# Attention steps placed by a list scheduler inside the kernel, with more of the splits on GpSimd

## Chip, core and metric

The kernel runs on one core of a Trainium2 chip. The metric is device time in microseconds (us) of one execution. The engines are TensorE (PE, its weight loads PEld), VectorE (DVE), ScalarE (ACT), GpSimd (POOL) and SyncE (SP, which issues nearly all DMAs here).

## The reference

```python
scores = (q @ k.T) / 8                       # batch 4, 8 heads, 576 x 576, head size 64
scores = where(scores >= max(scores) - tau, scores, -1e9)
attn = exp(scores - max(scores)); attn /= sum(attn) + 1e-9
x = attn @ v                                 # as 2304 tokens x 512
x = (silu(x @ w_gate) * (x @ w_val)) @ w_out        # inner width 1536
out = ((x @ w1) * (x @ w2) @ w3) @ w_out2           # inner width 1024
```

All inputs are float32. Products are made in a rounded format, so each operand is split into a rounded part hi and a remainder lo, and two or three products are added.

## The kernel before

The program has two stretches. The first is attention; the second, the two feed-forward blocks, is not touched.

Attention goes over 16 pairs of heads (p = 0 to 15), and a pair over nine score tiles (i = 0 to 8). For a tile, `mm_scores` multiplies four times (eight for i = 4) into one of two PSUM score banks (`s_bank`). `el_tile` then runs, on DVE, the pass L473, which copies the tile to SBUF as E and accumulates its extreme, the small add L477, which adds tau to that extreme (128x1, both inputs in SBUF), and the pass L481, which masks by the threshold and writes P (E comes from SBUF, the other input from the score bank). The exponential L485 follows on ACT. A score bank is free again after L481.

From P, ten banks of a pair are turned: four by `it_T(p, 0, c)`, one each by `it_lq` and `it_kl`, four by `it_T(p, 1, c)`. A turn is four transposes on PE (L327) into one of four `t_bank`s. `evac_split` takes hi and lo out of the bank by one of three paths: X (ACT copies hi, DVE subtracts, L505 and L507), Z (ACT copies hi L497, PE subtracts hi in the bank L334, ACT copies lo L501), Y (ACT copies the bank to SBUF L518, POOL rounds it L102 and subtracts L105). The paths come in rotation, `PATHS = "XZYXZZYXZ"`. A small corner bank goes by ACT and DVE.

`it_pv` multiplies the values, once for each head and half: eight products with `AT` (L566) and two with `ATL` (L571) into one bank, all ten emitted together; ACT copies the result (L578), and SP stores it (L582). AT and ATL exist once, so a pair's turns into them wait for the value products of the pair before.

For the next pair, `turn` transposes q and k; ACT takes hi (L342), DVE lo (L344), and `stack` (L350, L351) issues 12 DMAs on SP, eight for L (q) and four for R (k), which the next pair's scores read. `it_left` prepares the left-over rows.

The order comes from two queues of closures: before and after each tile, `some(0.5)` takes closures from `main` and `prep` by credits.

```python
def some(frac):
    credit[0] += 19.5 / 9 * frac
    credit[1] += (1.5 if in_tail else 1.0) * frac
    for c, qu in ((1, prep), (0, main)):
        while credit[c] >= 1 and qu:
            credit[c] -= 1
            run_item(qu.popleft())
```

The instructions emitted so are placed on the engines by the framework's own scheduler, which may change their order. Three early weight conversions (pairs 3, 6, 9) also run in this stretch.

Of the kernel before, what the change touches and what calls it, by code (L numbers as in the profile page):

```python
# [30 lines left out]

PATHS, LAST = "XZYXZZYXZ", "XZ"


@with_exitstack
def kernel(
# [62 lines left out]
    def split_pool(hi, lo, src):  # L101
# [2 lines left out]
        )  # L104
        nc.gpsimd.tensor_tensor(out=lo, in0=src, in1=f32(hi), op=ALU.subtract)  # L105

    def split_act_pool(hi, lo, src):
        nc.scalar.copy(out=hi, in_=src)  # L108
        nc.gpsimd.tensor_tensor(out=lo, in0=src, in1=f32(hi), op=ALU.subtract)  # L109
# [20 lines left out]
        nc.sync.dma_start(out=dst, in_=src)  # L130
        return raw

    def conv_bits(raw):
# [16 lines left out]
        nc.scalar.activation(out=a, in_=x, func=ACTF.Relu, scale=8.0, bias=ebias[:, 0:1])  # L150
        nc.scalar.activation(out=x, in_=x, func=ACTF.Relu, scale=-8.0, bias=ebias[:, 1:2])  # L151
        nc.gpsimd.tensor_tensor(out=a, in0=a, in1=x, op=ALU.subtract)  # L152
        return a, m

    def conv_value(bits):
        if wide == 1:
            return bits
        a, m = bits
# [76 lines left out]
    def attention(actx, early, tail):  # L235
# [23 lines left out]
        def load_left(b):  # L259
            qk = ld.tile([P, H, D], F32, tag="qkl", name="qkl", bufs=1)  # L260
            vl = ld.tile([P, HP, D], F32, tag="vl", name="vl", bufs=1)
            nc.sync.dma_start(out=qk[0:64], in_=q[b, :, 512:S, :].rearrange("h p d -> p h d"))
            nc.sync.dma_start(out=qk[64:128], in_=k[b, :, 512:S, :].rearrange("h p d -> p h d"))
            vs = v[b, :, 512:S, :].rearrange("(g e) p d -> e p g d", e=2)
            for e in range(2):
                nc.sync.dma_start(out=vl[64 * e:64 * e + 64], in_=vs[e])
            lraw[b] = (qk, vl)

        def load(p, which):
            b, hp = divmod(p, HP)  # L270
            for i in which if p < NP else ():
                src = (q, k, v)[i][b, 2 * hp:2 * hp + 2, 0:512, :]
                if i == 2:
                    t = wk.tile([P, 2, 4, D], F32, tag="ld2", name="ld2")
                    nc.sync.dma_start(out=t, in_=src.rearrange("h (p t) d -> p h t d", t=4))
                else:
                    t = ld.tile([P, 4, 2, D], F32, tag=f"ld{i}", name=f"ld{i}")
                    if p == 0:
                        t = t.rearrange("p (h a) b d -> p h (a b) d", h=2)
                        nc.sync.dma_start(out=t, in_=src.rearrange("h (p t) d -> p h t d", t=4))  # L280
                    else:
                        nc.sync.dma_start(out=t, in_=src.rearrange("h (p t) d -> p t h d", t=4))
                raws[p, i] = t
# [167 lines left out]
        def p_tile(p, i):  # L451
            if (p, 0) not in pbuf:
                for t in range(4):
                    pbuf[p, t] = pb[p % 2].tile([P, 2 * S], F32, tag=f"P{t}", name=f"P{t}")
                pbuf[p, 4] = pb[p % 2].tile([P, S], F32, tag="P4", name="P4")
            if i == 4:
                return pbuf[p, 4]
            h, t = (0, i) if i < 4 else (1, i - 5)
            return pbuf[p, t][:, h * S:(h + 1) * S]
# [4 lines left out]
                sums[b] = wk.tile([P, NSM], F32, tag="sums", name="sums")  # L464
            return stats[b]

        def el_tile(p, i, sb):
            st = stat(p // HP)
            c = slice(col_of(p, i), col_of(p, i) + 1)
            src = sb[:, :, 0:HALF]  # L470
            halves = lambda t: t.rearrange("p (a c) -> p a c", a=2)
            t = wk.tile([P, S], F32, tag="E", name="E", bufs=N_E)
            nc.vector.tensor_scalar(  # L473
                out=halves(t), in0=src, scalar1=-FAR, scalar2=None,
                op0=ALU.mult, op1=ALU.min, accum_out=st[:, 0, c],
            )
# [4 lines left out]
            nc.vector.scalar_tensor_tensor(  # L481
                out=halves(u), in0=halves(t), scalar=st[:, 1, c], in1=src,
                op0=ALU.is_gt, op1=ALU.subtract,
            )
            nc.scalar.activation(  # L485
                out=u, in_=u, func=ACTF.Exp, scale=-FAR, bias=st[:, 0, c],
                accum_out=sums[p // HP][:, c],
            )


        path_i = [0]

        def evac_split(hi, lo, bank):
            path = LAST[path_i[0] % len(LAST)] if in_tail else PATHS[path_i[0] % len(PATHS)]
            path_i[0] += 1
            if path == "Z":
                nc.scalar.copy(out=hi, in_=bank)  # L497

                def rest():
                    less(bank, hi)  # L500
                    nc.scalar.copy(out=lo, in_=bank)  # L501

                deferred.append(rest)
            elif path == "X":
                nc.scalar.copy(out=hi, in_=bank)  # L505
                deferred.append(
                    lambda: nc.vector.tensor_tensor(  # L507
                        out=lo, in0=bank, in1=f32(hi), op=ALU.subtract
                    )
                )  # L510
            else:
                raw = tmp()
                rv = raw
                if len(bank.shape) == 3:
                    rv = raw.rearrange("p (a c) -> p a c", a=bank.shape[1])
                if len(bank.shape) == 4:
                    rv = raw.rearrange("p (c h q) -> p c h q", c=4, h=2)
                nc.scalar.copy(out=rv, in_=bank)  # L518
                if path == "Y":
                    split_pool(hi, lo, rv)  # L520
                else:
                    nc.scalar.copy(out=hi, in_=bank)
                    nc.gpsimd.tensor_tensor(out=lo, in0=rv, in1=f32(hi), op=ALU.subtract)
# [89 lines left out]
        def split_items(p):  # L613
            return [lambda: split_left(p // HP)] if p % HP == 0 else []
# [46 lines left out]
        def stage_s(n):  # L661
            if n < NS:
                banks[n] = mm_scores(*tiles[n])

        def stage_el(n):
# [4 lines left out]
            if i == 8:  # L670
                main.extend(b_items(p))

        credit = [0.0, 0.0]

        def some(frac):
            credit[0] += 19.5 / 9 * frac
            credit[1] += (1.5 if in_tail else 1.0) * frac
# [3 lines left out]
                    run_item(qu.popleft())  # L681
                credit[c] = min(credit[c], 1.0)

        stage_s(0)
        stage_s(1)
        for n, (p, i) in enumerate(tiles):
            b, hp = divmod(p, HP)
            if i == 0:
                if p + 2 < NP:
                    if (p + 2) % HP == 0:  # L690
                        load_left((p + 2) // HP)
                    load(p + 2, (1, 0))
                while prep:
                    run_item(prep.popleft())
                if p + 1 < NP:
                    prep.extend(prep_items(p + 1))
                    credit[1] = 0.0 if p else -1.5
            if i == NTILE - 2:
                while prep:
                    run_item(prep.popleft())  # L700
                if p + 2 < NP:
                    prep.extend(split_items(p + 2))
            some(0.5)
            stage_el(n)
            stage_s(n + 2)
            some(0.5)
            if i == 4 and p in EARLY:
                prep.extend([conv_step, conv_end])
            if n + NTILE == NS:
                in_tail.append(True)  # L710
                lctx.close()
                prep.extend(early())
            if n + 2 == NS:
                while main:
                    run_item(main.popleft())
                qctx.close()
                prep.extend(tail())
# [382 lines left out]
```

## Time and profile before

| what | value |
|---|---|
| median of three runs | 1192.82 us (1192.11 to 1193.11) |
| profiled execution | 1192.23 us, span 1190.4 us |
| granted TensorE clock, mean | 0.987 |
| busy share of the span: PE, PEld, DVE, ACT, POOL | 94%, 80%, 63%, 50%, 32% |
| first L473 of pair 2, of pair 15 | 56.33 us, 340.51 us |

Busy time is the union of an engine's instructions; "idle before" is the time in which the engine did nothing before an instruction, and the arrow names what ended it. Inside an engine, consecutive instructions overlap a little, so a step from start to start can be shorter than a duration.

### The profile page before, as it was taken

The page shows a single profiled execution, that of the slowest core. Times are in us where ns is not written, and L with a number is a line of the kernel's source. Part 1 is how long each engine was busy: PE and PEld are TensorE (multiplying, and loading weights), DVE is VectorE, ACT ScalarE, POOL GpSimd, SP SyncE. Part 2 cuts the span into 40 slices and gives each one's busy share as a digit, 9 for nine tenths or more (in the row PEclk, how much of TensorE's full clock was granted, in tenths as well). Part 3 has the DMA queues.
Part 4 walks back from the last instruction along what each step waited for, and adds up shares of the span by engine and source line. Part 5 has one row for each costly group of instructions (what it writes and reads, how often), then busy time and mean ns, then how long its engine had stood idle before and what let it go on. Part 6 is the DMA issues. An engine that isn't in the chain of part 4 may idle for free.

```text
span 1190.4 us, 16901 instructions
## 1 busy us (share of the span) xinstructions
PE 1124.1 (94%) x6044; PEld 955.8 (80%) x6044; DVE 753.5 (63%) x1319; ACT 596.5 (50%) x1187; POOL 384.4 (32%) x353
## 2 busy tenths in 40 slices
PE   5998888899889889999999999999899999999998
PEld 4887778787777678888888888888787888888886
DVE  6888898889987797666464564577892022432222
ACT  4888888888876546443242432345563331321111
POOL 3234233233232655444232342234241131321210
PEclk9999999999998999999999999999899999999999
DMA  9675665665545653222021120123330010100014
GB/s 208 153 159 141 145 166 130 155 141 122 123 138 144 198 151 108 88 71 70 20 71 36 36 89 1 53 83 109 120 111 22 1 36 1 36 1 1 1 57 103
DMA packets 105331, 107.09 MB, mean 90 GB/s; under 512 B 48288, under 2 KB 79648, under 8 KB 105248
## 3 DMA queue, kind: packets, MB, share of 16 engines
q1 hardware_dynamic: 105104, 106.01, 33.4%
q8 instruction: 48, 0.79, 0.3%
q14 instruction: 35, 0.29, 0.1%
q10 hardware_dynamic: 144, 0.00, 0.0%
HBM read 68.16 MB, written 14.23 MB: 69 GB/s over the span
## 4 chain that ended last, share of the span: by engine, by line
PE 71%; DVE 15%; ACT 5%; DMA 3%; issue 3%; SPq 1%; POOL 0%; DVEq 0%; ACTq 0%; POOLq 0%
PE t_bank L804 37%; PE s_bank L804 19%; PE t_bank L566 5%; PE s_bank L441 5%; PE t_bank L327 3%; DVE E L473 3%; DVE P L481 2%; DMA raw<-in_moe_w_dram 2%; DVE slot L787 2%; ACT P L485 1%; DVE stat L477 1%; PE t_bank L571 1%; DVE raw L144 1%; DVE tmp L147 1%; DVE tmp L159 1%
## 5 line engine op out<-in xcount | busy, mean ns | idle before, releaser
L804 PE MATMUL t_bank<-slot,slot 128*128 128x512 f32 (+1 forms) x2592 | 561.2, 371 | 5.0 <-DVE slot L787 2.8
L804 PEld LDWEIGHTS t_bank<-slot,slot 128*128 128x128 f32 x2592 | 457.4, 189 | 92.4 <-DVE slot L787 4.0
L804 PE MATMUL s_bank<-h,slot 128*128 128x512 f32 (+1 forms) x720 | 164.1, 376 | 3.6 <-ACT h L108 2.9
L804 PEld LDWEIGHTS s_bank<-h,slot 128*128 128x128 f32 x720 | 128.4, 192 | 28.5 <-ACT h L108 3.4
L152 POOL TENSOR_TENSOR raw<-raw 128x512 int32<-128x512 int32 x76 | 83.3, 1096 | 170.8 <-ACT raw L151 157.8
L1036 DVE TENSOR_TENSOR tmp<-tmp,t_bank 128x512 f32<-128x512 f32 (+1 forms) x40 | 25.3, 633 | 178.2 <-PE t_bank L804 178.2
L473 DVE TENSOR_SCALAR_CACHE_REDUCE E<-s_bank 128x576 f32<-128x576 f32 x144 | 107.0, 752 | 32.9 <-PE s_bank L441 32.2
L485 ACT ACTIVATE P<-P,stat 128x576 f32<-128x576 f32 x144 | 113.5, 789 | 23.9 <-DVE P L481 23.4
L109 POOL TENSOR_TENSOR h<-tmp,h 128x512 fp32r<-128x512 f32 (+1 forms) x60 | 75.6, 1260 | 141.9 <-ACT h L108 137.0
L481 DVE SCALAR_TENSOR_TENSOR P<-E,stat,s_bank 128x576 f32<-128x576 f32 x144 | 114.5, 808 | 1.5
L441 PE MATMUL s_bank<-R,L 128*128 128x288 f32 x512 | 99.0, 317 | 16.0 <-DVE P L481 10.9
L327 PE MATMUL t_bank<-ident,P 128*128 128x128 f32 x640 | 98.4, 282 | 14.6 <-ACT P L485 7.8
L1040 POOL TENSOR_TENSOR h<-tmp,h 128x512 fp32r<-128x512 f32 (+1 forms) x38 | 45.8, 1205 | 200.5 <-ACT h L1038 200.5
L804 PE MATMUL s_bank<-slot,h 128*128 128x512 f32 x432 | 106.6, 391 | 0.9 <-DVE slot L1026 0.8
L889 DVE TENSOR_TENSOR tmp<-tmp,t_bank 128x512 f32<-128x512 f32 (+1 forms) x60 | 37.9, 631 | 108.2 <-PE t_bank L804 101.1
L441 PEld LDWEIGHTS s_bank<-R,L 128*128 128x128 f32 x512 | 76.3, 195 | 27.5 <-issue 9.4
L327 PEld LDWEIGHTS t_bank<-ident,P 128*128 128x128 f32 x640 | 75.8, 143 | 27.0 <-ACT P L485 14.0
L804 PEld LDWEIGHTS s_bank<-slot,h 128*128 128x128 f32 x432 | 80.0, 188 | 18.3 <-DVE slot L1026 2.1
L851 DVE TENSOR_TENSOR slot<-s_bank,slot 128x1024 f32<-128x1024 f32 (+1 forms) x72 | 82.4, 1146 | 18.6 <-PE s_bank L804 16.5
L159 DVE SCALAR_TENSOR_TENSOR tmp<-tmp,raw 128x512 f32<-128x512 f32 x76 | 68.2, 899 | 33.4 <-POOL raw L152 33.3
L888 ACT ACTIVATE tmp<-t_bank 128x512 f32<-128x512 f32 (+1 forms) x60 | 33.3, 555 | 109.7 <-PE t_bank L804 103.3
L150 ACT ACTIVATE raw<-raw,ebias 128x512 int32<-128x512 int32 x76 | 58.1, 764 | 58.0 <-DVE tmp L147 44.5
(106 smaller groups left out, 1406.6 us busy)
## 6 DMA issues: line engine op xcount, KB each, us to landing
raw<-in_moe_w_dram SPq DMA_DIRECT2D x32, 512.0 KB, 3.6
raw<-in_moe_w_out_dram SPq DMA_DIRECT2D x20, 512.0 KB, 3.5
x_dram<-xs SPq DMA_DIRECT2D x64, 144.0 KB, 2.4
L<-qlo SPq DMA_DIRECT2D x60, 128.0 KB, 2.4
L<-qhi SPq DMA_DIRECT2D x60, 128.0 KB, 3.0
raw<-in_moe_w_gate_dram SPq DMA_DIRECT2D x12, 512.0 KB, 3.7
raw<-in_moe_w_val_dram SPq DMA_DIRECT2D x12, 512.0 KB, 3.5
ld<-in_k_dram SPq DMA_DIRECT2D x16, 256.0 KB, 3.5
```

The costliest lines, as they stand in the source:

```text
L109: nc.gpsimd.tensor_tensor(out=lo, in0=src, in1=f32(hi), op=ALU.subtract)
L150: nc.scalar.activation(out=a, in_=x, func=ACTF.Relu, scale=8.0, bias=ebias[:, 0:1])
L152: nc.gpsimd.tensor_tensor(out=a, in0=a, in1=x, op=ALU.subtract)
L159: nc.vector.scalar_tensor_tensor(out=f32(m), in0=f32(m), scalar=2.0 ** 20, in1=f32(a), op0=ALU.add, op1=ALU.mult)
L327: nc.tensor.matmul(bank[:, t * P:(t + 1) * P], lhsT=part, rhs=ident, is_transpose=True, start=(t == 0), stop=(t == len(parts) - 1),)
L441: nc.tensor.matmul(o, lhsT=lhs, rhs=R[:, c:c + HALF], start=(h == hs2[0] and e == 0), stop=(h == hs2[-1] and e == 1),)
L473: nc.vector.tensor_scalar(out=halves(t), in0=src, scalar1=-FAR, scalar2=None, op0=ALU.mult, op1=ALU.min, accum_out=st[:, 0, c],)
L481: nc.vector.scalar_tensor_tensor(out=halves(u), in0=halves(t), scalar=st[:, 1, c], in1=src, op0=ALU.is_gt, op1=ALU.subtract,)
L485: nc.scalar.activation(out=u, in_=u, func=ACTF.Exp, scale=-FAR, bias=st[:, 0, c], accum_out=sums[p // HP][:, c],)
L566: nc.tensor.matmul(o, lhsT=vs[:, 4 * h + c, :, :].rearrange("p a d -> p (a d)"), rhs=AT[h][:, e, c, cs], start=(c == 0 and e == 0), stop=F ...
L804: nc.tensor.matmul(o, lhsT=lhs(a), rhs=rhs(c), start=(first and i == 0), stop=(last and i == 2))
L851: nc.vector.tensor_tensor(out=a, in0=s, in1=a, op=ALU.add)
```

## The change

A class `Plan` collects attention as steps. A step has an engine, a busy time, a time until its result is seen, the steps that it depends on, and a due time in units of tiles; it may open or close a bank or a `tmp` buffer. `order` is a list scheduler: it simulates the engines with these numbers and takes, again and again, the step that can start first, among equals the one due first. The steps of pairs 0 to 14 (and the first two score tiles of pair 15) are emitted in that order inside `tc.manual_schedule()`, so that each engine issues them in the order of emission. Pair 14's later turns and values, and pair 15, go as before.

Other differences: the ten banks of a pair go by the fixed row `"YZYYYXYYZX"` (six Y, two Z, two X) in place of the rotation; value products are three steps (four, four, two) in place of ten in a row; the passes of two neighbouring tiles have due times that put both L473 passes, then both small adds, then both L481 passes; the small add is a `tensor_scalar` with tau as a per-partition scalar in place of a `tensor_tensor`.

```diff
-PATHS, LAST = "XZYXZZYXZ", "XZ"
+ROWS, LAST = ("YZYYYXYYZX",), "XZ"
+class Plan:
+    ROOM = {"bank": 4, "tmp": N_TMP}
+    HOP, AHEAD = 0.06, 60
...
+        while any(queues.values()):
+            best = None
+            for engine, q in queues.items():
+                ready = []
+                for due, k, step in q[:self.AHEAD]:
+                    t = earliest(step, free[engine])
+                    if t is not None:
+                        ready.append((t, due, k, step))
+                if not ready:
+                    continue
+                first = min(r[0] for r in ready)
+                t, due, k, step = min(
+                    (r for r in ready if r[0] <= first), key=lambda r: r[1:3]
+                )
+                if best is None or t < best[0]:
+                    best = (t, engine, due, k, step)
...
-            nc.vector.tensor_tensor(
-                out=st[:, 1, c], in0=st[:, 0, c], in1=tau_sb, op=ALU.add
-            )
+        def el_thr(p, i):
...
+            nc.vector.tensor_scalar(
+                out=st[:, 1, c], in0=st[:, 0, c], scalar1=tau_sb, scalar2=None, op0=ALU.add
+            )
...
+        def plan_turn(p, i, due, deps):
...
+            d = plan.add("DVE", 0.66 if i == 0 else 0.6, 0.74, [c], lo, due + 0.3, closes=b)
+            def then():
...
+            return plan.add("SP", 0.5, 3.0, [d], then, due + 0.4)
...
+        def plan_evac(path, b, a, due, hi, lo):
+            if path == "Y":
...
+                c = plan.add("ACT", 0.47, 0.6, [a], raw, due + 0.1, opens=r, closes=b)
+                d = plan.add(
+                    "POOL", 0.59, 0.63, [c], lambda: pool_round(hi, k["r"]), due + 0.2
+                )
+                e = plan.add(
+                    "POOL", 1.25, 1.3, [d], lambda: pool_rest(lo, k["r"], hi), due + 0.2,
+                    closes=r,
+                )
+                return [d, e]
...
+        def plan_pv(p, h, n, due, deps, mid_deps, last_deps):
...
+            x = plan_bank(b, due, 0.53, deps, start)
+            y = plan.add("PE", 0.53, 0.7, [x] + mid_deps, lambda: part((2, 3)), due)
+            z = plan.add("PE", 0.27, 0.44, [y] + last_deps, end, due)
...
+        def make_plan():
...
+                    score[n] = plan.add("PE", big, big + 0.17, deps, go, n - 3)
...
+                    two = n - n % 2
+                    a = plan.add("DVE", 0.675, 0.75, [score[n]], mx, two)
+                    c = plan.add("DVE", 0.12, 0.2, [a], lambda p=p, i=i: el_thr(p, i), two + 0.1)
+                    mask[n] = plan.add(
+                        "DVE", 0.72, 0.81, [c] + war,
+                        lambda n=n, p=p, i=i: el_mask(p, i, banks.pop(n), es.pop(n)), two + 0.2)
+                    ex[n] = plan.add(
+                        "ACT", 0.77, 0.79, [mask[n]], lambda p=p, i=i: el_exp(p, i), n + 0.5)
...
+                rk = plan_turn(q, 1, z + (1.5 if p else 3), soon + ready[p][:1])
+                rq = plan_turn(q, 0, z + (3 if p else 4), soon + ready[p][1:2])
...
+                for c in range(4):
+                    a, e = plan_T(
+                        p, z + 5 + 0.6 * c, row[c], P0, old[:2],
...
+                        pv[p, h, n] = plan_pv(
+                            p, h, n, z + 12 + 1.6 * h + 0.8 * n,
...
-        stage_s(0)
-        stage_s(1)
-        for n, (p, i) in enumerate(tiles):
...
+        make_plan()
+        with tc.manual_schedule():
+            for step in plan.order():
+                if step["emit"] is not None:
+                    step["emit"]()
...
+        for n, (p, i) in list(enumerate(tiles))[PL:]:
             some(0.5)
             stage_el(n)
             stage_s(n + 2)
             some(0.5)
-            if i == 4 and p in EARLY:
-                prep.extend([conv_step, conv_end])
```

Here z is 9p, the number of the pair's first tile.

## Rows read from the trace of the kernel before

**Rows 1.** The page's busy tenths in 40 slices of the span.
```profile
DVE  6888898889987797666464564577892022432222
```

**Rows 2.** Windows: pair 0, pairs 2 to 14, after attention; busy us per engine.
```profile
core 0: us, PE busy (x) PEld busy (x) DVE busy (x) ACT busy (x) POOL busy (x), PEclk, DMA share, GB/s
17.30:35.35 18.05, 12.80 (x70) 11.33 (x68) 15.31 (x39) 10.78 (x28) 2.75 (x4) 0.81 0.93 238
56.33:340.51 284.18, 254.91 (x1805) 225.69 (x1803) 250.59 (x570) 237.19 (x567) 98.92 (x107) 0.99 0.61 142
...
383.00:1190.40 807.40, 791.05 (x3770) 661.54 (x3768) 424.42 (x581) 292.40 (x475) 254.67 (x210) 0.99 0.20 62
```

**Rows 3.** Groups by line and form, 56.33 to 340.51: busy, mean ns | idle before.
```profile
L473 DVE TENSOR_SCALAR_CACHE_REDUCE E<-s_bank 128x576 f32<-128x576 f32 x118 | 87.6, 752 | 27.4 <-PE s_bank L441 26.8
...
L105 POOL TENSOR_TENSOR AT<-tmp,AT 128x512 fp32r<-128x512 f32 x26 | 33.7, 1295 | 2.2
L501 ACT CAST AT<-t_bank 128x512 fp32r<-128x512 f32 x53 | 31.2, 602 | 0.9 <-PE t_bank L334 0.7
...
L477 DVE TENSOR_TENSOR stat<-stat,tau_sb 128x1 f32<-128x1 f32 x117 | 30.7, 271 | 1.2
L507 DVE TENSOR_TENSOR AT<-t_bank,AT 128x512 fp32r<-128x512 f32 x39 | 26.6, 684 | 0.4 <-ACT AT L505 0.2
...
L102 POOL TENSOR_SCALAR AT<-tmp 128x512 fp32r<-128x512 f32 x26 | 16.5, 633 | 81.2 <-ACT tmp L518 81.2
```

**Rows 4.** DVE's timeline, 128 to 134 us: start, us, instruction, idle before.
```profile
128.28 0.75 DVE L473 TENSOR_SCALAR_CACHE_REDUCE E<-s_bank 128x576 f32<-128x576 f32 x1
...
128.95 0.75 DVE L473 TENSOR_SCALAR_CACHE_REDUCE E<-s_bank 128x576 f32<-128x576 f32 x1
...
129.62 0.28 DVE L477 TENSOR_TENSOR stat<-stat,tau_sb 128x1 f32<-128x1 f32 x2
129.82 1.53 DVE L481 SCALAR_TENSOR_TENSOR P<-E,stat,s_bank 128x576 f32<-128x576 f32 x2
133.06 0.76 DVE L473 TENSOR_SCALAR_CACHE_REDUCE E<-s_bank 128x576 f32<-128x576 f32 x1 [1.70 <-PE s_bank L441]
```

**Rows 5.** The chain that ended last, 128 to 137 us: start, us, what.
```profile
128.71 0.30 PE t_bank L419 x4
129.01 1.13 PE t_bank L566 x8
130.14 0.27 PE t_bank L571 x2
...
131.73 0.23 PE t_bank L334
131.96 1.05 PE s_bank L441 x8
...
136.19 0.45 PE t_bank L327 x4
```

**Rows 6.** Timeline of all engines from 205.5 us: DVE and POOL.
```profile
205.89 1.33 DVE L477 TENSOR_TENSOR stat<-stat,tau_sb 128x1 f32<-128x1 f32 x2
205.93 1.27 POOL L105 TENSOR_TENSOR AT<-tmp,AT 128x512 fp32r<-128x512 f32 x1
```

**Rows 7.** Timeline of all engines from 489.2 us, in a weight conversion: POOL and DVE.
```profile
489.29 1.30 POOL L201 TENSOR_TENSOR slot<-tmp,slot 128x512 fp32r<-128x512 f32 x1 [1.28 <-ACT slot L198]
...
489.62 1.25 DVE L141 TENSOR_SCALAR tmp<-raw 128x512 int32<-128x512 int32 x1
...
490.90 0.43 DVE L144 TENSOR_SCALAR raw<-raw 128x512 int32<-128x512 int32 x1
```

**Rows 8.** SP's timeline, first and last of eight copies into L.
```profile
124.89 0.70 SPq L351 DMA_DIRECT2D L<-qhi  x1
...
130.16 0.60 SPq L351 DMA_DIRECT2D L<-qhi  x1
```

**Rows 9.** The page's DMA issues: copies from issue to landing.
```profile
L<-qlo SPq DMA_DIRECT2D x60, 128.0 KB, 2.4
```

More of the change, by code (lines that the diff above doesn't have):

```diff
@@ L105, in split_pool, with pool_round, pool_rest @@
         nc.gpsimd.tensor_tensor(out=lo, in0=src, in1=f32(hi), op=ALU.subtract)
+    def pool_round(hi, src):
+        nc.gpsimd.tensor_scalar(
+            out=hi, in0=src, scalar1=1.0, scalar2=1.0, op0=ALU.mult, op1=ALU.mult
+        )
+    def pool_rest(lo, src, hi):
+        nc.gpsimd.tensor_tensor(out=lo, in0=src, in1=f32(hi), op=ALU.subtract)
     def split_act_pool(hi, lo, src):
@@ L149, in conv_bits, with conv_power, conv_less @@
         )
[L150 to L153, printed above, removed]
+        return a, m, x
+    def conv_power(bits):
+        if wide == 2:
+            a, m, x = bits
+            nc.scalar.activation(out=a, in_=x, func=ACTF.Relu, scale=8.0, bias=ebias[:, 0:1])
+            nc.scalar.activation(out=x, in_=x, func=ACTF.Relu, scale=-8.0, bias=ebias[:, 1:2])
+    def conv_less(bits):
+        if wide == 2:
+            a, m, x = bits
+            nc.gpsimd.tensor_tensor(out=a, in0=a, in1=x, op=ALU.subtract)
+    def conv_bits(raw):
+        bits = conv_mantissa(raw)
+        conv_power(bits)
+        conv_less(bits)
+        return bits
     def conv_value(bits):
@@ L157, in conv_value @@
             return bits
-        a, m = bits
+        a, m, _ = bits
         nc.vector.scalar_tensor_tensor(
@@ new lines, in plan_left, with fill, out @@
+        def plan_left(p, due, deps):
+            b = plan.res("bank")
+            bt, hp = divmod(p, HP)
+            def fill(bank):
+                qk_tiles(p)
+                br = bank.bitcast(F32R)
+                for e in range(2):
+                    for h in range(2):
+                        c = (2 * e + h) * P
+                        s0 = (e + h + 1) % 2
+                        src = lsplit[bt][:, 2 * hp + h, s0:s0 + 2, :]
+                        nc.tensor.transpose(
+                            br[:, c:c + P], src.rearrange("p a d -> p (a d)"), ident_r
+                        )
+            a = plan_bank(b, due, 0.28, deps, fill)
+            def out():
+                L, R = qk_tiles(p)
+                lz = LZ.rearrange("p e (h c) -> p e h c", c=192)[:, :, :, 0:64]
+                bv = b["t"].rearrange("p (e h c) -> p e h c", e=2, h=2)
+                scaled(lz, bv[:, :, :, 0:64], q_scale)
+                scaled(R[:, 512:640].rearrange("p (h c) -> p h c", h=2), bv[:, 1, :, 64:P])
+                scaled(R[:, 2 * S:2 * S + 64], bv[:, 1, 1, 64:P])
+            return plan.add("ACT", 0.8, 0.95, [a], out, due + 0.1, closes=b)
@@ new lines, in plan_T, with fill, plan_corner @@
+        def plan_T(p, due, path, deps, war, cols, dst, shape=None):
+            b = plan.res("bank")
+            def fill(bank):
+                turn_p(bank, cols())
+                if shape:
+                    b["t"] = bank.rearrange(shape, c=4, h=2)
+            a = plan_bank(b, due, 0.44, deps + war, fill)
+            return [a], plan_evac(path, b, a, due, *dst)
+        def plan_corner(p, due, deps, war):
+            b = plan.res("bank")
+            def fill(bank):
+                nc.tensor.transpose(bank[:, 0:P], pbuf[p, 4][:, 448:S], ident)
+                nc.tensor.transpose(bank[0:64, 64:64 + P], pbuf[p, 4][:, 512:S], ident)
+            a = plan_bank(b, due, 0.22, deps + war, fill)
+            hi = ATL[:, 0, 512:S]
+            c = plan.add(
+                "ACT", 0.1, 0.23, [a],
+                lambda: nc.scalar.copy(out=hi, in_=b["t"][:, 64:P]), due + 0.1,
+            )
+            d = plan.add(
+                "DVE", 0.13, 0.21, [c], lambda: nc.vector.tensor_tensor(
+                    out=ATL[:, 1, 512:S], in0=b["t"][:, 64:P], in1=f32(hi), op=ALU.subtract
+                ), due + 0.3, closes=b,
+            )
+            return [a], [c, d]
@@ new lines, in plan_pv, with part, start, end @@
+        def plan_pv(p, h, n, due, deps, mid_deps, last_deps):
+            bt, hp = divmod(p, HP)
+            b = plan.res("bank")
+            cs = slice(n * HALF, (n + 1) * HALF)
+            def part(cc):
+                for c in cc:
+                    for e in range(2):
+                        nc.tensor.matmul(
+                            b["t"][:, 0:HALF],
+                            lhsT=splits[p, 2][:, 4 * h + c, :, :].rearrange("p a d -> p (a d)"),
+                            rhs=AT[h][:, e, c, cs], start=(c == 0 and e == 0), stop=False,
+                        )
+            def start(bank):
+                b["t"] = bank
+                part((0, 1))
+            def end():
+                for e in range(2):
+                    nc.tensor.matmul(
+                        b["t"][:, 0:HALF],
+                        lhsT=VLZ[bt % 2][:, hp, h, :, :].rearrange("p a d -> p (a d)"),
+                        rhs=ATL[:, e, cs], start=False, stop=(e == 1),
+                    )
+            x = plan_bank(b, due, 0.53, deps, start)
+            y = plan.add("PE", 0.53, 0.7, [x] + mid_deps, lambda: part((2, 3)), due)
+            z = plan.add("PE", 0.27, 0.44, [y] + last_deps, end, due)
+            def out():
+                if n == 0:
+                    xs_t[p, h] = wk.tile([P, S], F32, tag="xs", name="xs", bufs=2)
+                nc.scalar.copy(out=xs_t[p, h][:, cs], in_=b["t"][:, 0:HALF])
+            o = plan.add("ACT", 0.3, 0.4, [z], out, due + 0.1, closes=b)
+            if n == 1:
+                g = 2 * hp + h
+                def store():
+                    xs = xs_t.pop((p, h))
+                    for e in range(2):
+                        nc.sync.dma_start(
+                            out=x_dram[e, g * D:(g + 1) * D, bt, :],
+                            in_=xs[64 * e:64 * e + 64, :],
+                        )
+                plan.add("SP", 0.15, 3.0, [o], store, due + 0.2)
+            return z
@@ new lines, in plan_norm, with sums_of, out, store @@
+        def plan_norm(b, due, deps):
+            k, bk = {}, plan.res("bank")
+            def sums_of():
+                k["r"] = wk.tile([P, NSM], F32, tag="r", name="r")
+                nc.vector.tensor_scalar(
+                    out=k["r"], in0=sums[b], scalar1=1e-9, scalar2=None, op0=ALU.add
+                )
+                nc.vector.reciprocal(out=k["r"], in_=k["r"])
+            a = plan.add("DVE", 0.5, 0.6, deps, sums_of, due)
+            c = plan_bank(
+                bk, due, 0.11, [a],
+                lambda bank: nc.tensor.transpose(bank[0:NSM, 0:P], k["r"], ident),
+            )
+            def out():
+                k["rt"] = wk.tile([NSM, P], F32, tag="rt", name="rt")
+                nc.scalar.copy(out=k["rt"], in_=bk["t"][0:NSM, 0:P])
+            d = plan.add("ACT", 0.2, 0.3, [c], out, due + 0.1, closes=bk)
+            def store():
+                nc.sync.dma_start(
+                    out=r_dram[b, :, 0:512].rearrange("h (t c) -> h t c", c=P),
+                    in_=k["rt"][0:4 * H, :],
+                )
+                nc.sync.dma_start(
+                    out=r_dram[b, :, 512:S].rearrange("(g h) c -> g h c", h=2),
+                    in_=k["rt"][4 * H:NSM, :].rearrange("g (h c) -> g h c", h=2),
+                )
+            plan.add("SP", 0.2, 3.0, [d], store, due + 0.2)
@@ new lines, in plan_split_left, with qk_round @@
+        def plan_split_left(b, due, war):
+            k = {}
+            def qk_round(e):
+                if not k:
+                    k["qk"], k["vl"] = lraw.pop(b)
+                    lsplit[b] = sp.tile([P, H, 3, D], F32R, tag="qkls", name="qkls", bufs=1)
+                pool_round(lsplit[b][:, :, e, :], k["qk"])
+            a = plan.add("POOL", 0.59, 0.63, war, lambda: qk_round(0), due)
+            c = plan.add("POOL", 0.59, 0.63, [a], lambda: qk_round(2), due)
+            d = plan.add("POOL", 1.25, 1.3, [c], lambda: pool_rest(
+                lsplit[b][:, :, 1, :], k["qk"], lsplit[b][:, :, 0, :]), due)
+            last = [d]
+            for h in range(2):
+                r = slice(64 * h, 64 * h + 64)
+                hi, lo = (VLZ[b % 2][r, :, h, e, :] for e in range(2))
+                last.append(plan.add(
+                    "POOL", 0.38, 0.43, [last[-1]],
+                    lambda hi=hi, r=r: pool_round(hi, k["vl"][r]), due + 6 + h))
+                last.append(plan.add(
+                    "POOL", 0.72, 0.76, [last[-1]],
+                    lambda hi=hi, lo=lo, r=r: pool_rest(lo, k["vl"][r], hi), due + 6 + h))
+            return d, last[-1]
@@ new lines, in plan_split_v, with first_half, rest @@
+        def plan_split_v(p, due, war):
+            def first_half():
+                splits[p, 2] = wk.tile([P, 8, 2, D], F32R, tag="sp2", name="sp2")
+                pool_round(splits[p, 2][:, :, 0, :], raws[p, 2].rearrange("p h t d -> p (h t) d"))
+            def rest():
+                raw = raws.pop((p, 2)).rearrange("p h t d -> p (h t) d")
+                pool_rest(splits[p, 2][:, :, 1, :], raw, splits[p, 2][:, :, 0, :])
+            a = plan.add("POOL", 0.59, 0.63, war, first_half, due)
+            c = plan.add("POOL", 1.25, 1.3, [a], rest, due)
+            if p + 2 < NP:
+                plan.add("SP", 0.1, 3.0, [c], lambda: load(p + 2, (2,)), due + 0.1)
+            return c
@@ new lines, in plan_conv, with begin, end @@
+        def plan_conv(due):
+            k, r = {}, plan.res("tmp")
+            def begin():
+                conv_fetch()
+                k["raw"], *k["rest"] = conv_raw.popleft()
+                k["bits"] = conv_mantissa(k["raw"])
+            def end():
+                conv_fetch()
+                k["val"] = conv_value(k["bits"])
+            a = plan.add("DVE", 1.7, 1.8, [], begin, due, opens=r)
+            c = plan.add("ACT", 1.1, 1.3, [a], lambda: conv_power(k["bits"]), due + 0.2)
+            d = plan.add("POOL", 1.0, 1.05, [c], lambda: conv_less(k["bits"]), due + 0.4)
+            e = plan.add("DVE", 0.6, 0.68, [d], end, due + 1)
+            f = plan.add("ACT", 0.47, 0.6, [e], lambda: k["rest"][0](k["val"]), due + 1.2)
+            plan.add("POOL", 1.25, 1.3, [f], None, due + 1.4, closes=r)
@@ L673, in attention @@
+        lefts = {}
         credit = [0.0, 0.0]
@@ L682, in some @@
                 credit[c] = min(credit[c], 1.0)
-        stage_s(0)
-        stage_s(1)
-        for n, (p, i) in enumerate(tiles):
[L687 to L702, printed above, removed]
+        make_plan()
[3 more added lines that the diff above has]
+                    step["emit"]()
+        late = NP - 2
+        main.append(lambda: it_kl(late))
+        main.extend(lambda c=c: it_T(late, 1, c) for c in range(4))
+        main.extend(lambda h=h, n=n: it_pv(late, h, n) for h in range(2) for n in range(2))
+        for n, (p, i) in list(enumerate(tiles))[PL:]:
             some(0.5)
```

241 lines of the change are left out of this document (232 added, 9 removed).

## The prediction

> **What bounds the kernel now.** I read the page's busy tenths first: DVE is at 8 or 9 in slices 2 to 12, which are attention, and at 7 or less in most of the others [rows 1]. So the change acts on a stretch where DVE is nearly full. The windows then give its size [rows 2]: pairs 2 to 14 take 284.18 us, which is 21.86 a pair, and inside a pair the busy times are DVE 250.59/13 = 19.28, PE 19.6, ACT 18.2, POOL 7.6. The 807 us behind attention have PE busy for 98% and are not edited; I carry them over unchanged.
>
> No engine is full, so the order matters. DVE sits idle for 21.86 − 19.28 = 2.58 a pair, and the groups say for whom: 26.8 of the 27.4 us before L473, 2.06 a pair, end with a score product on PE [rows 3]. One instance shows how it comes about. DVE waits 1.70 us for a tile's scores [rows 4]; meanwhile the chain shows PE in two heads' worth of value products, from 129.01 on, and the scores start only at 131.96 [rows 5]. PE goes strictly in its order, so a score whose bank is free stands behind 1.40 us blocks of value products. PE itself needs, by the same chain rows, 10 x 0.53 for scores (tile 4 counts twice), 4 x 1.40 for values, 12 x 0.45 for turns, some 0.5 for the corner and the left-over rows (0.30 of it the latter's four), and 0.23 for each Z: 17.8 of 21.86.
>
> A second loss is inside DVE's busy time. The small add L477 takes 0.14 us where two run freely [rows 4], but 0.271 on the mean [rows 3]. Where it is long, POOL is at work: two adds take 1.33 us, and the POOL subtraction that starts at nearly the same moment 1.27 [rows 6]. That is 9 x 0.12 = 1.1 us a pair. L473 and L507, which read PSUM, keep 0.752 and 0.684.
>
> **The change, part by part, for one pair.**
>
> Paths. The rotation gives ten banks 3.33 X, 4.44 Z and 2.22 Y; the new row 2, 2 and 6. DVE loses 1.33 subtractions of 0.68 [rows 3]: −0.9. PE loses 2.44 corrections of 0.23 [rows 5]: −0.55, leaving 17.3. ACT has one copy for X and Y and two for Z; 2.44 of 0.60, of which some 0.1 overlaps: −1.2, leaving 17.0. POOL gains 3.78 times 0.63 + 1.29 [rows 3]: +7.3, so 14.9 in place of 7.6. That is not free: it is hidden only as long as POOL's 14.9 fit under the others, and as long as nobody waits for POOL.
>
> The small add becomes a one-input instruction. If that frees it from POOL, DVE loses the 1.1. The trace of before has no `tensor_scalar` on a 128x1 tile beside POOL work, so the cost is bounded: below 0.14 each as when undisturbed, above the full wait of rows 6. I take the lower end, because the passes nearest in time and tile, with one SBUF input at most, are not prolonged by POOL.
>
> So DVE is busy for 19.28 − 0.9 − 1.1 = 17.3. Pairing the tiles can only lower that (two tiles from 128.28 to 131.35 are 1.5 each [rows 4]); I count nothing for it, since many tiles go in twos already.
>
> Order. Value products in steps of four, four and two leave at most 0.53 us of PE work in front of a score. On average a ready score then waits for half of that, 0.27, in each of 4.5 rounds of two tiles: 1.2 us. Beside it I keep the 0.5 of DVE idle time that is not for scores today. DVE idle: 1.7, with 0.5 as the lower bound (every wait filled by a subtraction or a q or k remainder) and today's 2.58 as the upper.
>
> Sum: 17.3 + 1.7 = 19.0 a pair, between 17.8 and 19.9. PE at 17.3, ACT at 17.0 and POOL at 14.9 fit under 19.0, though with three engines near 90% it is nearer the upper end than an even bound would put it.
>
> SP. The planner books 0.5 us for the eight copies into L; the trace has the first at 124.89 and the last ending at 130.76: 5.9 us [rows 8]. At the same rate the pair's 12 stack copies, four stores and three loads hold SP for some 14 of 19.0 us. That is no bound, but it is a wrong number in the plan.
>
> Total: pairs 1 to 14 took 340.51 − 35.35 = 305.2, 21.8 each; at 19.0 they save 39. Pair 0 (18.05, DVE busy 15.31 [rows 2]) can save at most its 2.7 idle; I take 1. From the profiled execution's 1192.2, which stands 0.6 below the median: 1192.2 − 40 = **1152**. With 17.8 and 19.9 a pair, and pair 0 the same, 1135 to 1165.
>
> **Rivals.**
>
> *A, slower: the small add still waits for POOL.* Another one-input `tensor_scalar` between SBUF tiles does wait: L141 starts 0.33 after a POOL subtraction and takes 1.25, ending just behind it; its like L144 takes 0.43 with POOL idle [rows 7]. The Trainium skill (SBUF — State Buffer, "Who interferes with whom") says that a `tensor_scalar` in a two-port mode takes a port pair that DVE shares with GpSimd, and the later of the two blocks fully. The trace agrees at L141; by that rule the new add could wait as the old one did, if one element suffices for the mode, which no row here shows. From rows: POOL busy goes from 34.8% [rows 2] to some 75%, and if the waits grow in proportion, 1.1 becomes 2.4 a pair; 19.0 + 2.4 = 21.4, and 1186. If arrivals are random, because POOL's six splits stand back to back, each add waits 0.75 x half of 1.27 = 0.47: 4.3 a pair, 23.3, +21 in all, so about 1212. It decides at 21.8 − 19.0 = 2.8 a pair, 0.31 us an add. For it: L141. Against: L141's kind does 512 elements in 0.43 us where L507 needs 0.68 [rows 3], so it runs in a faster way, from which a single column has nothing to gain.
>
> *B, L comes late.* SP's copies into L land 2.4 us after issue [rows 9]. Transposed a third into the pair (due z+3), q's last copy is issued near 6.3 + 2 + 5.9 and lands at 16.6 us, while the next pair's first score is wanted two tiles ahead, at 14.8 to 16.9. If it costs 2 us a pair, 21.0 and 1180. Against: a pair's first score needs only two of L's four blocks, and the turns of q may well start sooner than their due time.
>
> *C, the plan packs to its own sums.* If remainders fill the DVE waits and pairing saves another 0.5, the pair falls to about 17.5, where PE is full: 305.2 − 14 x 17.5 = 60, and with pair 0 some 1131; between this and the main case's 1135 lies nothing that I could tell apart.
>
> *D, no better order on the chip.* A planned order that meets other durations stalls as today's does: idle 2.6, 19.9, 1165. This is the upper end of my main case.
>
> **Numbers.** Main case with D, 1135 to 1166: 0.52. C, below 1135: 0.14. B, 1166 to 1185: 0.10. A mild, about 1186: 0.12. A hard, above 1195: 0.10. Anything else slower, such as POOL's queue delaying AT for the next pair: 0.02. The range that leaves out about 2 in 10 takes in most of C and A mild: 1132 to 1190. A change of 0.2% is about what this kernel's measurement can tell from none. Faster by more: main, C, B and most of A mild, 0.84; within: 0.04; slower: 0.12.
>
> **What will show it.** Right: pairs 2 to 14 near 19 us; DVE busy near 17.3 a pair; the new small add at 0.15 us with no long tail; idle before L473 falling from 2.06 a pair towards 1.3; POOL at 75 to 80%. Wrong by A: the small add at 0.4 us or more, with its long cases beside L105's successor. Wrong by B: score products or their weight loads waiting for DMAs into L at the pair's start. Wrong by an engine that becomes the bound: ACT or PE busy for all but 0.5 us of a pair, at under 18 us. The stretch behind attention should keep its 807 us within 2; if it does not, the prediction misses something that lies outside these steps.

## The result, and the profile after

The changed kernel takes 1175.3 us (median of four, 1174.3 to 1176.5) against 1192.5: a ratio of 0.9856, 95% interval 0.9839 to 0.9873. That is 17 us faster. I had forecast 40, so the direction was right, and well over half of the gain did not come.

The windows of the changed kernel, with the columns of [rows 2]: pair 0, pair 1, pairs 2 to 14, pair 15 with its end, and behind attention.

```profile
15.52:36.77 21.25, 13.89 (x77) 12.18 (x77) 14.77 (x36) 11.12 (x28) 7.70 (x9) 0.97 0.37 83
36.77:62.24 25.47, 19.96 (x134) 18.81 (x132) 21.97 (x47) 15.97 (x37) 11.13 (x12) 0.89 0.74 186
62.24:321.72 259.48, 238.11 (x1764) 225.81 (x1765) 234.62 (x550) 218.33 (x531) 188.10 (x206) 0.97 0.67 156
...
364.00:1173.20 809.20, 791.78 (x3775) 663.12 (x3773) 424.04 (x581) 292.33 (x477) 254.00 (x210) 0.99 0.21 62
```

Set against the forecast, the 23 us that are missing lie here. Pairs 2 to 14 take 259.48/13 = 19.96 each, not 19.0: 12.5 us. Pair 1 takes 25.5: 6.5 us. Pair 0 was to shrink from 18.05 to 17.05 and grew to 21.25; it starts 1.8 earlier, which leaves 2.4. From pair 15's first tile to the end it is 851.5 against 849.9: 1.6. The stretch behind attention kept its 807 within 2, as forecast.

Per pair of 2 to 14, DVE is busy for 18.05 (19.28 before, 17.3 forecast) and idle for 1.91 (2.58 before, 1.7 forecast). PE is at 18.3 (17.3 forecast), ACT at 16.8 (17.0), POOL at 14.5 (14.9).

The groups of pairs 2 to 14 that answer to [rows 3], with the same columns:

```profile
L571 DVE TENSOR_SCALAR_CACHE_REDUCE E<-s_bank 128x576 f32<-128x576 f32 x117 | 87.3, 752 | 21.2 <-PE s_bank L539 20.1
...
L580 DVE TENSOR_SCALAR stat<-stat,tau_sb 128x1 f32<-128x1 f32 x117 | 22.7, 209 | 1.4
```

The wait for scores fell from 26.8 to 20.1 us, 2.06 to 1.55 a pair. The small add fell from 0.271 to 0.209. Its line over the whole run, with minimum, median and maximum in ns, shows how:

```profile
L580 DVE TENSOR_SCALAR stat<-stat,tau_sb x144: 195/208/216, 17.2 to 346.8; 128x1 f32<-128x1 f32 x144
```

No add of 144 is long, though POOL is busy for 188.10 of 259.48 us. Rival A is out. But the add also takes 0.06 more than the 0.15 which I had put in.

Two stalls stand out. The first is DVE's timeline at the end of pair 1:

```profile
55.37 0.21 DVE L580 TENSOR_SCALAR stat<-stat,tau_sb 128x1 f32<-128x1 f32 x1
57.71 0.81 DVE L225 TENSOR_SCALAR tmp<-raw 128x512 int32<-128x512 int32 x1 [2.12 <-DMA raw<-in_moe_w_gate_dram]
58.56 1.36 DVE L228 TENSOR_SCALAR raw<-raw 128x512 int32<-128x512 int32 x1
...
61.51 0.80 DVE L587 SCALAR_TENSOR_TENSOR P<-E,stat,s_bank 128x576 f32<-128x576 f32 x1
```

L225, L228 and L231 (left out here) are the weight conversion that belongs to pair 3. Its step has no dependency, so the planner could put it into an early idle time of DVE, two pairs ahead. There DVE waits for the load, works for 3.8 us (booked: 1.7), and the mask L587, whose add ended at 55.58, stands behind it until 61.51. No score bank comes free meanwhile. PE's timeline shows the next score product waiting for that mask, and windows around it, with the columns of [rows 2], show what that does to PE:

```profile
62.37 0.91 PE L539 MATMUL s_bank<-R,L 128*128 128x288 f32 x4 [4.15 <-DVE P L587]
```
```profile
58.00:62.30 4.30, 0.22 (x2) 0.00 (x0) 4.27 (x5) 0.68 (x1) 3.04 (x3) 1.00 0.98 279
62.30:64.00 1.70, 1.63 (x8) 1.17 (x9) 1.59 (x7) 1.67 (x4) 0.00 (x0) 0.68 0.59 119
64.00:66.00 2.00, 2.00 (x11) 2.00 (x10) 1.78 (x6) 2.00 (x6) 1.78 (x3) 0.50 0.59 131
```

PE does 0.22 us of work in 4.3, and behind it its granted clock (third last column) falls to 0.50, the lower of its two levels, for some 3 us.

The second stall is at the start of pair 10. First SP's copies into L, the first and last of eight; then PE's timeline; then DVE's:

```profile
218.33 0.46 SPq L448 DMA_DIRECT2D L<-qlo  x1
...
224.28 0.59 SPq L449 DMA_DIRECT2D L<-qhi  x1
```
```profile
225.59 0.66 PE L539 MATMUL s_bank<-R,L 128*128 128x288 f32 x3 [1.67 <-DMA L<-qlo]
```
```profile
226.29 0.76 DVE L571 TENSOR_SCALAR_CACHE_REDUCE E<-s_bank 128x576 f32<-128x576 f32 x1 [3.71 <-PE s_bank L539]
```

The copies hold SP for 6.5 us and the last issue ends 1.4 before the pair's first tile; the score product waits for them, and DVE 3.71 for the product. That is the mechanism of rival B, to which I had given 0.10. Over pairs 2 to 14, score products wait for copies into L for 3.3 us in all, and their weight loads for 3.6.

### The profile page after: what moved, and what is told of

Its sections match the earlier page's. It is cut to its first block, busy times and chain, and to the rows that moved or that the text cites. A ratio compares the mean times of both kernels' runs of the same rounds, so it can differ in the third digit from the quotient of the medians.

```text
span 1173.2 us, 16903 instructions
## 1 busy us (share of the span) xinstructions
PE 1106.8 (94%) x6008; PEld 957.4 (82%) x6008; DVE 736.4 (63%) x1300; ACT 577.1 (49%) x1151; POOL 485.5 (41%) x463
## 4 chain that ended last, share of the span: by engine, by line
PE 55%; DVE 5%; DMA 1%; issue 1%; ACT 0%; POOL 0%; DVEq 0%; ACTq 0%
PE t_bank L1327 36%; PE s_bank L1327 19%; DMA raw<-in_moe_w_dram 1%; DVE tmp L257 1%; DVE slot L1310 1%; DVE raw L228 1%; DVE tmp L231 1%; DVE tmp L225 0%; DVE slot L1403 0%; DVE slot L299 0%; DVE slot L1512 0%; DVE slot L1374 0%; PE t_bank L1400 0%; DVE slot L1549 0%; POOL slot L299 0%
## 5 line engine op out<-in xcount | busy, mean ns | idle before, releaser
L1559 DVE TENSOR_TENSOR tmp<-tmp,t_bank 128x512 f32<-128x512 f32 (+1 forms) x40 | 25.3, 633 | 178.2 <-PE t_bank L1327 178.2
L539 PE MATMUL s_bank<-R,L 128*128 128x288 f32 x512 | 101.1, 323 | 20.9 <-DVE P L587 11.4
L587 DVE SCALAR_TENSOR_TENSOR P<-E,stat,s_bank 128x576 f32<-128x576 f32 x144 | 114.5, 809 | 1.6
L189 POOL TENSOR_TENSOR AT<-tmp,AT 128x512 fp32r<-128x512 f32 x88 | 113.3, 1303 | 1.8
L425 PE MATMUL t_bank<-ident,P 128*128 128x128 f32 x640 | 93.7, 281 | 4.6 <-ACT P L596 2.0
L1327 PEld LDWEIGHTS s_bank<-slot,h 128*128 128x128 f32 x432 | 80.0, 188 | 18.3 <-DVE slot L1549 2.1
L184 POOL TENSOR_SCALAR AT<-tmp 128x512 fp32r<-128x512 f32 x88 | 55.2, 639 | 91.5 <-ACT tmp L878 84.3
```

Source lines behind the costliest of these rows:

```text
L425: nc.tensor.matmul(bank[:, t * P:(t + 1) * P], lhsT=part, rhs=ident, is_transpose=True, start=(t == 0), stop=(t == len(parts) - 1),)
L539: nc.tensor.matmul(o, lhsT=lhs, rhs=R[:, c:c + HALF], start=(h == hs2[0] and e == 0), stop=(h == hs2[-1] and e == 1),)
L587: nc.vector.scalar_tensor_tensor(out=halves(p_tile(p, i)), in0=halves(t), scalar=st[:, 1, c], in1=sb[:, :, 0:HALF], op0=ALU.is_gt, op1=ALU ...
L1327: nc.tensor.matmul(o, lhsT=lhs(a), rhs=rhs(c), start=(first and i == 0), stop=(last and i == 2))
```

## The experiments

Each ratio is to the kernel before on the same chip. Differences in us are between medians taken on four occasions, on which the kernel before had 1191.3 to 1193.1; they are good to 1 or 2 us. What is said of single pairs comes from one profiled execution of each kernel.

**Moving q and k forward** (`q_early`), in the changed kernel:

```diff
-rk = plan_turn(q, 1, z + (1.5 if p else 3), ...)
-rq = plan_turn(q, 0, z + (3 if p else 4), ...)
+rk = plan_turn(q, 1, z + (0 if p else 3), ...)
+rq = plan_turn(q, 0, z + (0.5 if p else 4), ...)
```

> Only the due times of the two q and k transposes move: k from z+1.5 to z+0, q from z+3 to z+0.5 (pairs from 1 on). In the changed kernel the last copy into L is issued only 2 to 7 us before the next pair's first tile, and at eight pair starts the first score product begins 0.8 to 2.9 us after the pass that frees its bank. Theory L (copies into L come late, because the plan books 0.5 us for eight copies that take 5): the last copy is issued 8 us or more ahead, these waits go, and the total falls by 8 to 14 us, to 1161 to 1167. Theory C (the loss is the early weight conversions that stand in DVE's order two pairs too early): within 2 us of 1175. Theory M (no single cause; planned order meets other durations): within 4 us of 1175, the waits move elsewhere.

1168.0 us, 0.9782 (0.9751 to 0.9813): 7.4 less than the change. At pair 10 the eight copies now lie from 210.27 to 215.31, and its first tile follows at 221.73 with 0.69 of idle time before it. The wait goes as theory L says, but the gain ends just short of its range of 8 to 14. The first conversion has moved on: pair 1 takes 18.6 in place of 25.5, and pair 2 takes 26.9 in place of 20.2, with DVE waiting 4.3 us for the conversion's load.

**True costs for SP** (`sp_true`): the booked times of SP's steps alone, five of them; the first is shown.

```diff
-return plan.add("SP", 0.5, 3.0, [d], then, due + 0.4)
+return plan.add("SP", *((5.2, 7.6) if i == 0 else (2.6, 5.0)), [d], then, due + 0.4)
...
```

> Only the costs that the plan books for SP steps change: eight copies into L 5.2 us until 7.6 (was 0.5 until 3.0), four into R 2.6 until 5.0, two stores 1.2, loads 1.4 and 0.65. Due times stay. Theory L: the plan now knows when L is ready, orders other PE work before the first scores, and the total falls by 3 to 10 us, to 1165 to 1172, less than by an earlier start since the copies still land late. Theory C and theory M: within 4 us of 1175 either way.

1166.5, 0.9778 (0.9753 to 0.9803), inside theory L's range. The plan gains as much from knowing the price as from the earlier due times, and no score product of pairs 2 to 14 waits for a copy into L any more.

**Conversions in their own pairs** (`conv_dep`):

```diff
-a = plan.add("DVE", 1.7, 1.8, [], begin, due, opens=r)
+a = plan.add("DVE", 1.7, 1.8, deps, begin, due, opens=r)     # deps = [mask[z + 5]]
...
+conv_fetch()                                                 # before the planned region
```

> The three early weight conversions may begin only behind the mask of tile 5 of their own pair (3, 6, 9), and their first loads are issued before the planned region. In the changed kernel they stand in DVE's order in pairs 1, 4 and 7, the first waits 2.12 us for its load with a mask pass behind it, and these pairs take 25.5, 25.3 and 22.0 us. Theory C: pairs 1, 4, 5 and 7 fall to about 19.5 and the total by 10 to 15 us, to 1160 to 1165. Theory L: only the 2.1 us wait and some port waits go, 2 to 6 us, to 1169 to 1173. Theory M: within 3 us of 1175.

1163.3, 0.9752 (0.9728 to 0.9777): 12.0 less than the change, as theory C says. Pair 1 falls from 25.5 to 19.9, pairs 4, 5 and 7 from 25.3, 22.1 and 22.0 to 19.1, 18.1 and 20.6, and the pair with the first conversion, pair 3, takes 22.6. The dependency and the earlier first load were tested as one edit; no run parts them.

**The old small add** (`tt_add`), in the changed kernel: `tensor_tensor` with two SBUF inputs.

> Only the small add goes back to a tensor_tensor with two SBUF inputs; all else as changed, POOL busy for 72% of a pair. This prices what the one-input form is worth. If its waits grow with POOL's busy share, from 0.12 to 0.25 us an add (0.15 undisturbed): the add's mean is 0.35 to 0.45 us, DVE busy rises by 1.5 to 2.5 us a pair and the total by 15 to 35 us, to 1190 to 1210. If back-to-back POOL work makes each add wait 0.47 us: above 1205. If DVE has slack to take it: within 5 us of 1175.

1197.1, 1.0037 (1.0016 to 1.0059): 0.4% above the kernel before, and inside the first range. Its group for pairs 2 to 14, and its line over the run:

```profile
L580 DVE TENSOR_TENSOR stat<-stat,tau_sb 128x1 f32<-128x1 f32 x117 | 46.8, 410 | 1.4
```
```profile
L580 DVE TENSOR_TENSOR stat<-stat,tau_sb x144: 144/161/2575, 17.2 to 364.9; 128x1 f32<-128x1 f32 x144
```

0.41 on the mean, with a longest of 2.6 us: the waits of [rows 6], grown with POOL's share: over an undisturbed 0.15, some 0.12 us an add with POOL at 35% and 0.26 at 68%. The one-input form is worth 22 us here, more than the whole change gained.

**Repairs together** (`conv_q`: `conv_dep` and `q_early`; `conv_q_sp`: `sp_true` too).

> The edits of conv_dep (1163.3) and q_early (1168.0) together, costs of SP as in the changed kernel. If the two losses are separate stalls (conversions in pairs 1, 4, 7; late L at eight pair starts), the gains of 12.0 and 7.4 us add: 1154 to 1158, pairs 2 to 14 at 18.7 to 19.0 us. If both only remove the same slack, or the order is shuffled at random by any edit: 1160 to 1166.

1160.5, 0.9729 (0.9715 to 0.9744). The two give 14.8, not 19.4, which is in the second range. Its pairs 2 to 14, in the columns of [rows 2]:

```profile
56.83:304.59 247.76, 234.62 (x1773) 218.93 (x1772) 235.08 (x555) 217.95 (x534) 189.54 (x209) 1.00 0.73 166
```

That they remove the same slack does not follow. In the profiled executions the first tile of pair 15 starts at 321.7 in the changed kernel, 11.4 earlier in `conv_dep`, 6.7 in `q_early` and 17.1 in `conv_q`, so up to there the gains add but for 1 us. The rest of the gap lies behind that point and between the medians.

> conv_q and the true SP costs of sp_true (1166.5) together. If the true costs work by keeping L in time, they have little to add where q and k already go early: within 3 us of conv_q. If they work by a better order at large, another 4 to 8 us: 1147 to 1152.

1161.4, 0.9735 (0.9721 to 0.9750): nothing more. That is as it should be if the true costs work by having L in time.

**Parts alone in the kernel before.** `before_add` has only the one-input add, `before_paths` only `PATHS = "YZYYYXYYZX"`, `before_add_paths` both; none has the plan.

> The kernel before with one edit, the small add as the one-input tensor_scalar. Each add costs 0.228 us of DVE there, and in the changed kernel 0.163, which does not vary with POOL. If DVE's busy time is what counts: 0.065 x 9 = 0.6 us a pair, 8 to 10 us in all, 1181 to 1185. If the waits are hidden in DVE's slack: 1189 to 1194. If its worth in the kernel before is like that in the changed one (22 us): 1168 to 1175.

1191.7, 0.9982 (0.9965 to 0.9998): worth next to nothing, the second of the three expectations.

> The kernel before with the one-input add and the row of six Y, two Z, two X as its rotation; no plan, value products whole. My sum gives the paths 0.8 us of DVE, 0.55 of PE and 1.2 of ACT a pair. If they are worth that with the old order too: 1170 to 1178, at or under the changed kernel, and the plan has brought little. If the old order can't use them (POOL's remainders come later and AT with them): 1180 to 1195, and the gain of the change is the plan's.

1178.9, 0.9882 (0.9868 to 0.9897), between the two ranges. Its pairs 2 to 14:

```profile
54.24:324.71 270.47, 244.96 (x1774) 220.75 (x1775) 236.30 (x556) 221.16 (x532) 191.03 (x206) 0.99 0.64 149
```

That is 13.7 us less than in [rows 2]. The changed kernel needs another 11.0 less for these pairs (259.48), but its pair 2 starts at 62.24, 8.0 later than here.

> The kernel before with the row of six Y as its rotation and the old small add with two SBUF inputs. With the one-input add it was 1178.9, and the one-input add alone 1191.7. If the two edits only work together (the old add's waits grow with POOL's busy time, 35% to 70%): 0.23 becomes 0.35 to 0.40 of DVE an add, +1.7 to 2.2 us a pair, and 1195 to 1210. If the paths carry the gain by themselves: 1178 to 1184.

1194.2, 1.0020 (1.0003 to 1.0036), just under the first range. The add in `before_paths`, then the score pass in `before_add_paths`, pairs 2 to 14:

```profile
L477 DVE TENSOR_TENSOR stat<-stat,tau_sb 128x1 f32<-128x1 f32 x117 | 48.0, 423 | 1.4
```
```profile
L473 DVE TENSOR_SCALAR_CACHE_REDUCE E<-s_bank 128x576 f32<-128x576 f32 x118 | 87.8, 753 | 30.2 <-PE s_bank L441 29.3
```

Alone, the add brings 0.2% and the paths cost 0.2%; together they bring 1.2%. What DVE saves by six Y it loses again in the old add, 0.271 to 0.423, and DVE's busy time in pairs 2 to 14 even rises, from 250.59 to 257.42. The wait for scores is 29.3 us without the plan (26.8 in [rows 3]).

The total hides a part of this. In the profile of `before_add` pairs 2 to 14 take 277.09, 7.1 less than before, which is 0.55 a pair and what the shorter add accounts for; the stretch behind the last value product, which the edit does not touch, takes 813.8 against 808.1. In `before_paths` the pairs gain 3.4 and that stretch loses 3.5; with both edits it is back at 808.0. No run shows why, so how far the add's gain alone is lost by the edit, and how far by that stretch, is open.

**Parts undone in the repaired plan.** `conv_q_old_row` has the old rotation of paths, `conv_q_whole` a head's ten value products as one step.

> conv_q (1160.5; pairs 2 to 14 at 19.06) with the ten banks of a pair by the rotation of the kernel before (3.33 X, 4.44 Z, 2.22 Y) in place of six Y. My sum: DVE +0.8, PE +0.55, ACT +1.2 a pair; if the planned order keeps its idle time: 19.6 to 20.2 a pair, 1169 to 1177. If POOL's load is what holds the planned kernel: within 3 us of 1160 or below. If the planned order can only be had with the lighter engines: above 1180.

1172.2, 0.9832 (0.9797 to 0.9867), 19.7 us a pair, in the first range. With the one-input add, the paths are worth 11.7 under the plan.

> conv_q with a head's value products as one step of ten (1.33 us booked), behind all that they read. My sum gives the thirds 0.27 us of waiting in each of 4.5 rounds in place of 0.67: 1.8 us a pair at most, 25 us. If scores do wait behind whole blocks: 1170 to 1185, DVE's idle time before the score pass up by 0.5 to 1.8 a pair. If the planner just places the blocks where no score is due: 1158 to 1164.

1166.1, 0.9789 (0.9764 to 0.9814). The score pass in `conv_q`, then in `conv_q_whole`, pairs 2 to 14:

```profile
L571 DVE TENSOR_SCALAR_CACHE_REDUCE E<-s_bank 128x576 f32<-128x576 f32 x118 | 87.7, 753 | 9.5 <-PE s_bank L539 9.0
```
```profile
L571 DVE TENSOR_SCALAR_CACHE_REDUCE E<-s_bank 128x576 f32<-128x576 f32 x117 | 86.6, 754 | 18.2 <-PE s_bank L539 17.7
```

The thirds halve this wait, but pairs 2 to 14 are only 3.1 us shorter by them (247.76 and 250.88), 0.24 a pair in place of the 1.8 that I had as the most; the total is 5.6 less. That is between my two expectations, and nearer the second: that the planner places most whole blocks where no score is due fits, but no row here shows it.

**The start** (`conv_q_start`): `conv_q`, and the transposes of pair 1 no longer behind pair 0's third mask.

```diff
-soon = [score[z]] if p else [mask[2]]
+soon = [score[z]] if p else [None]
-landed[1, 0] = landed[1, 1] = mask[1]
+landed[1, 0] = landed[1, 1] = None
...
```

with due times z−3 and z−2.5 for k and q in pair 0.

> conv_q with the transposes of pair 1's q and k freed from the third mask of pair 0 and due first. In the planned kernels pair 0 takes 21 to 23 us (18.05 before), and pair 1's first score waits 3.3 to 4.9 for L, whose last copy is issued at 34.4 to 35.9 (26.9 before). If this is the late copy alone: pair 0 falls to 18 to 19, total 1156 to 1158. If pair 0 is held by something else: within 1.5 us of 1160.5.

**1154.0 us**, 0.9681 (0.9651 to 0.9711), the fastest of all and 2 under the first range. Its windows, pair 0, pair 1 and pairs 2 to 14:

```profile
15.40:32.66 17.26, 14.49 (x77) 13.14 (x76) 15.58 (x37) 10.82 (x27) 4.28 (x5) 1.00 0.79 175
32.66:50.14 17.48, 16.23 (x123) 15.20 (x122) 17.02 (x41) 14.17 (x37) 11.44 (x14) 1.00 0.55 124
50.14:299.03 248.89, 234.61 (x1773) 218.97 (x1772) 236.31 (x554) 218.01 (x534) 189.48 (x209) 1.00 0.72 166
```

Pairs 0 and 1 fall to 17.3 and 17.5 (23.0 and 18.5 in `conv_q`), and PE keeps the full clock (1.00 in all three).

## Why the prediction was half right

**What bounds.** Right. DVE and its wait for scores set the pair, and both fell.

**Paths.** Right in size for DVE, ACT and POOL. 26 subtractions in place of 43 over 13 pairs are 0.9 a pair less on DVE; ACT went down by 1.4 (I had 1.2), POOL up to 14.5 (14.9). PE was wrong: my 17.3 came from adding up single instructions, which gave 17.8 for the kernel before, where [rows 2] has it busy for 19.6. It is 18.3 in the changed kernel and 18.0 in `conv_q_start`, more than the 17.5 at which rival C had it full.

**The small add: a term mis-sized.** The sign and the mechanism were right, the term half: I took 1.1 a pair, and 9 x (0.271 − 0.209) is 0.56. The new form costs 0.209, not the 0.14 of the old one when undisturbed. I also missed that this is no separate term. The waits of rival A are what the paths bring with the old add; the sum added up two edits of which, in total time, each alone gains next to nothing.

**DVE busy, 17.3.** It is 18.05, and 0.75 a pair is 9.8 us over pairs 2 to 14. The add explains 0.5 of the 0.75; the rest I can't put on one line.

**Order, 1.7 idle.** The changed kernel's 1.91 is near it, but not for the reason in the sum. A good part of it is the two stalls: `conv_q`, without them, has 0.98, and `conv_q_start` 0.97, where scores are waited for only 0.68 a pair in place of my 1.2.

**Total: the step that failed.** The 23.0 us that are missing in the profiled execution are, in the terms of the sum, 9.8 for DVE busy, 2.7 for DVE idle, 8.9 for pairs 0 and 1, and 1.6 from pair 15 on. So two steps failed. One is the busy time, above all the add's 1.1. The other is that I multiplied a pair's sum by 14, gave pair 0 a gain of 1, and counted nothing for steps that the plan moves without its being their purpose. The runs show three of those. The conversions, which my sum does not mention, move two pairs forward: 12.0 us when undone alone. The copies into L, whose wrong price I did see and then called no bound, come late: 7.4 alone. The transposes for pair 1 start behind pair 0's third mask: 6.5, undone on top of the other two. Undone together they give 21.3.

That this leads to 1154.0, beside my 1152, is partly luck. In `conv_q_start` a pair takes 19.15 against my 19.0, but with DVE busy for 18.18 (17.3) and idle for 0.97 (1.7): two errors that cancel.

**Rivals.** A was false as stated. B's mechanism was there, but at some pair starts and not at every one, and it was worth 7.4 us and not 2 a pair; that the changed kernel's time lies in B's range is chance, since the conversions weigh more. D, as far as the pairs go, is what the changed kernel shows (19.96 against its 19.9), and in part for its reason: a conversion and the copies took longer than the plan had booked. But the stalls are in a few places: undoing two brings these pairs to 19.06.

**What stays open.** 5 us go from pair 15 on: from its first tile to the end, `conv_q_start` takes 854.9 where the kernel before took 849.9, about half of it ahead of the last value product and half behind. I have not tried what limits that hand-over.

As it was made, the plan with its thirds brought 3.6 us over `before_add_paths`, with intervals that overlap, because pairs 0 and 1 lost most of what pairs 2 to 14 gained; repaired, it brings 25.

## What to carry to other kernels

A step without a dependency can float to an early gap of a greedy planner, and with a fixed order the engine's other work then waits behind it for its data: give each step its true inputs (the load's landing among them), and each queue its measured price per issue, before judging the plan. When work is moved to an engine, test the move together with every instruction that waits for that engine, since two edits were worth 0.2% and −0.2% here by themselves and 1.2% together.

## What the runs showed of the hardware

A `tensor_scalar` on one column (128x1, both operands in SBUF) takes 0.195 to 0.216 us in the changed kernel, with POOL busy for 72% of pairs 2 to 14, while the `tensor_tensor` on the same column (`tt_add`) takes 0.144 at the least and up to 2.6. The 512-column `tensor_scalar` does wait: [rows 7], and L228 above with 1.36 beside a POOL subtraction from 58.21 to 59.64, where its like L144 takes 0.43 with POOL idle. So what the page "SBUF — State Buffer" of the Trainium skill ("Who interferes with whom") says of `tensor_scalar`, that it can contend with GpSimd, shows here at 512 columns, and not at one.
